# One-token attention over a long cache: each K and V load issued as two halves of its columns, one by SyncE and one by ScalarE

## The chip, the core and the metric

The kernel runs on one core of a Trainium2 chip. The core has a matrix engine (TensorE, PE in the profile), three elementwise engines (VectorE or DVE, ScalarE or ACT, GpSimd or POOL), and SyncE (SP), which here only issues DMAs. Each engine works through its own instruction queue in order; an instruction that waits on a semaphore holds everything behind it on that engine. DMA instructions stand in the same queues: SP's DMAs go to one hardware queue, ScalarE's to another, GpSimd's indirect DMAs to a third, and 16 DMA engines serve them.

The metric is the device time in microseconds (us) of one execution of the whole program. Times inside the program come from one profiled execution.

## What is computed

Two tokens (batch 2, width 512) pass a transformer block: layer norm, attention of one query position against caches of 8192 positions for 32 heads of width 128, an output projection with a residual, then a layer norm and an MLP of width 1792 with GELU, with a second residual. All is fp32. Cut to what matters:

```python
q = layernorm(x) @ wq                                # (2, 512) @ (512, 4096)
scores = einsum("bhqd,bhkd->bhqk", q, k_cache) * 128 ** -0.5
p = softmax(scores)                                  # over 8192 positions
o = einsum("bhqk,bhkd->bhqd", p, v_cache)
h = x + o.reshape(2, 4096) @ wo
out = h + mlp(layernorm(h))                          # 512 -> 1792 -> 512
```

K and V are 268 MB each; every byte is read once.

## The kernel before

**Tiles.** The work is cut into 32 steps `i` (`NI`), one for a pair of heads (`QG = 2`) and one batch entry. A step needs one K tile and one V tile, each 128 partitions by 128 positions (`NS`) by 128 floats: 64 KB of one partition, 8.39 MB in all. They come from one pool, `kv`, with three buffers (`BUFS = 3`), in the order wq, K0, V0, K1, V1, and so on. So V of step i+1 takes the buffer of K of step i and can be loaded once that K is used up; K of step i+2 takes the buffer of V of step i and can be loaded once the matmuls on that V are done. The last 'ws' tile in that pool holds the two MLP weights. All K and V loads are made by `load` (L70 to L76), called at L387, L394, L396, L409 and L411; before the change each is one DMA on SP. K of steps 30 and 31 is loaded in two parts (`parts_of`), V of step 31 in four.

**One step.** For K the tile is cut into four chunks `c` of 32 positions. VectorE multiplies a chunk in place by the query (L246). GpSimd halves part of it by an addition (L256), VectorE sums rows (L266); in the last three steps (`LAST`) ScalarE sums 38 of the 128 positions by activations with an accumulator (`by_act`, L260). When all 128 scores of each partition are there, the maximum is taken (L270), transposed on PE (L273), reduced (L277) and broadcast (L280); ScalarE makes the bias (L286) and the exponentials (L291, `exps`), and PE multiplies them with V (L314, `values`). ScalarE copies the result out (L320, `gather`).

**Around it.** Every second step, head outputs go into groups and meet rows of wo (`turn`, `turned`, L367). The groups' rows of wo are loaded by `load_wo`: five groups by a DMA on SP (L140; 1 MB, 1 MB, 1 MB, 0.5 MB and 0.25 MB), five by an indirect DMA from GpSimd (L145). The last pair's wo rows come by L412 (0.5 MB, tile 'wl' in the buffer of q). At the end: step 31 with its own order on PE (`stay_awake` L376 and `keep_warm` L515 are matmuls without use that fill gaps; `values(done, range(MOST))` L457 and the remainder of it L483), then the MLP (w1 by L468, w2 by L472).

**Order.** The framework that records the kernel decides each engine's order and adds the semaphore waits. Loads wait for the last users of their buffer. Completion of DMAs on the hardware queues is counted on eight semaphores taken in turn, so that a DMA also waits until the DMA eight before it, which has the same semaphore, has landed.

Of the kernel before, what the change touches and what calls it, by code (L numbers as in the profile page):

```python
# [41 lines left out]
def tile_decode_block(ctx: ExitStack, tc: tile.TileContext, x, k, v, wq, wo, w1, b1, w2, b2, out):  # L42
    nc = tc.nc
# [26 lines left out]
    def load(src, i, parts):  # L70
        m, b = divmod(i, B)
        t = kv.tile([P, NS, DH], F32, name="kv", tag="kv")
        rows = src[b, QG * m:QG * m + QG].rearrange("h (p j) d -> (h p) j d", j=NS)
        for s0, n in parts:
            nc.sync.dma_start(t[:, s0:s0 + n], rows[:, s0:s0 + n])
        return t  # L76

    wqt = kv.tile([P, DC, H * DH], F32, name="wqs", tag="kv")
# [16 lines left out]
    for blocks in PLAN:  # L95
        shut = blocks if isinstance(blocks, tuple) else None
        r = WR if shut else blocks
        n = (P - 4 * len(shut or ())) * r
# [286 lines left out]
    next_load = 0  # L385
    free_from = 1
    kt[0] = load(k, 0, cut(1))  # L387
    for i in range(NI):
        m, b = divmod(i, B)
        done = i - 1  # L390
        late = i == NI - 1
        if not late:
            if i < NI - 2:
                vt[i] = load(v, i, cut(1))  # L394
        else:
            vt[i] = load(v, i, [(0, 64), (64, 32), (96, 24), (120, 8)])  # L396
            b1r = rows2[:, 0].rearrange("p r q -> p (r q)")[:, :FN]
            nc.vector.memset(b1r, 0.0)
            b2s = rows2[:B, 1].rearrange("b r q -> b (r q)")
            for e in range(B):  # L400
                nc.sync.dma_start(b1r[WB * e::32], b1.rearrange("(n f) -> n f", n=NG))
            nc.sync.dma_start(b2s, b2[None, :].to_broadcast([B, D]))
# [248 lines left out]
```

## Time and profile before

| what | us |
|---|---|
| time, median of 3 runs (1307.66 to 1307.70) | 1307.67 |
| span of the profiled execution, first to last instruction | 1305.9 |
| VectorE busy | 932.7 (71%) |
| GpSimd busy | 494.2 (38%) |
| PE busy | 446.8 (34%) |
| ScalarE busy | 98.6 (8%) |
| SP's DMA queue, share of 16 DMA engines | 98.8% |
| read from memory | 562.32 MB, 431 GB/s over the span |

The profiled execution has no time of its own beside its span; the median is 1.77 us above the span. "PE so L314" is a matmul of line 314 that writes tile so; "SPq" and "ACTq" are DMA-issuing instructions of SP and ScalarE, whose lengths are those of the issue and not of the transfer. "x4" counts instructions merged in a row, and in square brackets stands how long the engine sat idle before and what ended that.

### The profile page before, as it was taken

Reading aid. Unit: us, or ns where it says so; the run is one execution under the profiler, and the core shown is the slowest. Engines: PE = TensorE matmul, PEld = TensorE weight load, DVE = VectorE, ACT = ScalarE, POOL = GpSimd, SP = SyncE. Lnnn points to the kernel's source line nnn. Section 1 sums busy time; section 2 is a strip of 40 time slices with the busy share of each in tenths; the row PEclk is TensorE's granted clock in tenths of the full one; section 3 lists DMA queues with packets and bytes.
Section 4 is the critical chain, followed back from the end, with each engine's and each line's share of the span. In section 5 each row is a group of like instructions: output and inputs, shape, how many; then the busy total and the mean of one; then the engine's idle time right before and its main releaser. Section 6 shows DMA issues by size and latency. Waiting matters only on the chain.

```text
span 1305.9 us, 7466 instructions
## 1 busy us (share of the span) xinstructions
PE 446.8 (34%) x2934; PEld 130.9 (10%) x2934; DVE 932.7 (71%) x551; ACT 98.6 (8%) x431; POOL 494.2 (38%) x151
## 2 busy tenths in 40 slices
PE   3033313333332334413342232333323334123468
PEld 0001001010010101001010010101001011000113
DVE  3666688757688666787766787666787667797891
ACT  0000000000000000000000000000000000004440
POOL 0433344532344432444332454333444433453330
PEclk9566556766566666656766566666666666566689
DMA  9999999999999999999999999999999999999998
GB/s 418 426 440 428 438 422 444 424 440 426 442 426 440 428 438 428 426 444 430 436 426 438 430 434 436 424 442 424 440 426 432 438 432 436 429 428 429 428 434 351
DMA packets 12727, 561.50 MB, mean 430 GB/s; under 512 B 1568, under 2 KB 1584, under 8 KB 2484
## 3 DMA queue, kind: packets, MB, share of 16 engines
q1 hardware_dynamic: 11968, 557.08, 98.8%
q0 software_dynamic: 720, 3.93, 0.7%
q8 instruction: 23, 0.38, 0.1%
q14 instruction: 12, 0.10, 0.0%
q10 hardware_dynamic: 4, 0.00, 0.0%
HBM read 562.32 MB, written 0.00 MB: 431 GB/s over the span
## 4 chain that ended last, share of the span: by engine, by line
DMA 43%; DVE 24%; issue 14%; PE 12%; POOL 5%; ACT 1%; SPq 0%; POOLq 0%; DVEq 0%
DMA kv<-in_A_k_cache_dram 38%; DVE kv L246 14%; PE so L314 10%; DVE s L266 9%; POOL kv L256 5%; DMA kv<-in_A_v_cache_dram 3%; DMA ws<-in_B_w_dram 1%; ACT pt L291 1%; PE rowacc L367 1%; DVE orow L350 1%; PE sm L280 1%; PE sm L273 0%; DVE gm L277 0%; DVE mx L270 0%; ACT nb L286 0%
## 5 line engine op out<-in xcount | busy, mean ns | idle before, releaser
L246 DVE TENSOR_TENSOR kv<-kv,qps 128x4096 f32<-128x4096 f32 x128 | 562.4, 4415 | 313.8 <-DMA kv<-in_A_k_cache_dram 313.6
L256 POOL TENSOR_TENSOR kv<-kv 128x2048 f32<-128x2048 f32 (+3 forms) x128 | 476.8, 3734 | 754.1 <-DVE kv L246 566.3
L266 DVE TENSOR_REDUCE s<-kv 128x32 f32<-128x2048 f32 (+5 forms) x160 | 325.3, 2066 | 10.9 <-POOL kv L256 10.6
L314 PE MATMUL so<-kv,pt 128*8 128x512 f32 x2048 | 280.8, 709 | 42.7 <-ACT pt L291 37.3
L273 PE MATMUL sm<-ident,mx 128*1 128x128 f32 x32 | 10.9, 340 | 446.0 <-DVE mx L270 446.0
L314 PEld LDWEIGHTS so<-kv,pt 128*8 128x8 f32 x2048 | 56.4, 101 | 239.5 <-issue 194.3
L367 PE MATMUL rowacc<-wog,ot 128*2 128x512 f32 x70 | 50.3, 881 | 64.8 <-DVE ot L365 33.4
L286 ACT ACTIVATE nb<-sm 128x2 f32<-128x2 f32 x32 | 5.5, 172 | 851.4 <-PE sm L280 851.4
L231 PE MATMUL qps<-q,pick 2*64 2x256 f32 x64 | 13.8, 577 | 127.6 <-DVE kv L246 127.6
L273 PEld LDWEIGHTS sm<-ident,mx 128*1 128x1 f32 x32 | 2.5, 79 | 472.5 <-issue 278.0
L358 PE MATMUL sm<-ident,orow 2*128 2x2 f32 x35 | 5.2, 244 | 130.1 <-DVE orow L350 130.1
L320 ACT ACTIVATE ss<-so 128x512 f32<-128x512 f32 x31 | 18.5, 598 | 269.6 <-PE so L314 269.6
L260 ACT ACTIVATE kv<-kv 128x128 f32<-128x128 f32 x114 | 33.5, 295 | 24.2 <-DVE kv L246 21.4
L335 PE MATMUL sm<-ss,selr 128*34 128x128 f32 x240 | 28.7, 273 | 0.0
L291 ACT ACTIVATE pt<-s,nb 64x128 f32<-64x128 f32 x64 | 25.5, 399 | 1.4
L335 PEld LDWEIGHTS sm<-ss,selr 128*34 128x34 f32 x240 | 25.1, 112 | 0.0
L260 ACT ACTIVATION_READ_ACCUMULATOR kv<-kv 128x1 f32 x114 | 21.3, 186 | 0.0
L280 PE MATMUL sm<-gm,ones 1*128 1x2 f32 x64 | 16.6, 326 | 11.9 <-DVE gm L277 11.9
L277 DVE TENSOR_REDUCE gm<-sm 1x2 f32<-1x128 f32 x32 | 8.9, 279 | 16.2 <-PE sm L273 16.2
L231 PEld LDWEIGHTS qps<-q,pick 2*64 2x64 f32 x64 | 5.5, 192 | 136.9 <-DVE kv L246 133.2
L358 PEld LDWEIGHTS sm<-ident,orow 2*128 2x128 f32 x35 | 4.4, 207 | 132.6 <-DVE orow L350 79.9
L367 PEld LDWEIGHTS rowacc<-wog,ot 128*2 128x2 f32 x70 | 6.8, 107 | 97.9 <-issue 64.1
(110 smaller groups left out, 169.2 us busy)
## 6 DMA issues: line engine op xcount, KB each, us to landing
kv<-in_A_k_cache_dram SPq DMA_DIRECT2D x4, 4096.0 KB, 32.9
ws<-in_B_w_dram SPq DMA_DIRECT2D x3, 1792.0 KB, 18.5
kv<-in_A_v_cache_dram SPq DMA_DIRECT2D x1, 4096.0 KB, 33.4
wog<-in_A_wo_dram SPq DMA_DIRECT2D x3, 1024.0 KB
kv<-in_A_v_cache_dram SPq DMA_DIRECT2D x1, 2048.0 KB, 37.9
kv<-in_A_v_cache_dram SPq DMA_DIRECT2D x1, 1536.0 KB, 41.2
ws<-in_B_w_dram SPq DMA_DIRECT2D x1, 1024.0 KB, 17.0
wog<-in_A_wo_dram SPq DMA_DIRECT2D x1, 512.0 KB
```

The costliest lines, as they stand in the source:

```text
L231: nc.tensor.matmul(t[e * HP:(e + 1) * HP, :, b], pick[32 * n:32 * n + B, b, :], rows[:, :, e], start=True, stop=True)
L246: return nc.vector.tensor_tensor(kc, kc, qb, op=ALU.mult)
L256: nc.gpsimd.tensor_tensor(t[:, :, :DH // 2], t[:, :, :DH // 2], t[:, :, DH // 2:], op=ALU.add)
L260: nc.scalar.activation(kt[i][:, j, :], kt[i][:, j, :], AF.Copy, accum_out=ST[i][:, j:j + 1])
L266: nc.vector.tensor_reduce(ST[i][:, a:e], kt[i][:, a:e, :d], axis=AX.X, op=ALU.add)
L273: nc.tensor.transpose(MT[i], mx, ident)
L280: GI[i] = nc.tensor.matmul(GM[i], ones[:1, :], gm, start=True, stop=True)
L291: nc.scalar.activation(ptz[i % 2][ps, :, 4 * e:4 * e + 4], s[ps], AF.Exp, bias=nb[ps, e:e + 1], scale=SCALE, accum_out=LT[m][ps, 32 * e + ...
L314: m = nc.tensor.matmul(so[32 * n:32 * n + 4 * QG], ptz[i % 2][:, u, :], vt[i][:, 4 * u:4 * u + 4, :], start=(u < NG), stop=(u >= NS // 4 - ...
L320: return nc.scalar.activation(SS[i], so2[i % 2], AF.Copy)
L335: nc.tensor.matmul(OP[m], sel_row[:, j, B - 1 - c:B - 1 - c + QR], SS[i - 1 + c][:, j * DH:(j + 1) * DH], start=(c == 0 and j == 0), stop= ...
L367: nc.tensor.matmul(rowacc, t[:, r, :], wo_g[g][:, r, :], start=False, stop=(g == len(groups) - 1 and r == n - 1))
```

## The change

In `load`, each part (columns s0 to s0+n of the tile) is cut in the middle. The first half is issued by SP, the second by ScalarE. The bytes, the tiles and the buffers stay the same. 64 loads in 69 DMAs become 138 DMAs, 69 in each of the two queues; one partition's piece of a whole load goes from 64 KB to 32 KB. All other DMAs stay where they were written.

```diff
         for s0, n in parts:
-            nc.sync.dma_start(t[:, s0:s0 + n], rows[:, s0:s0 + n])
+            mid = s0 + n // 2
+            nc.sync.dma_start(t[:, s0:mid], rows[:, s0:mid])
+            nc.scalar.dma_start(t[:, mid:s0 + n], rows[:, mid:s0 + n])
         return t
```

## The prediction

> **What bounds it now.** I read the page first: its DMA lines, then the windows for the rate, then the timeline around the landings of K, and last the chain and the timeline of the final 65 us.
>
> ```profile
> DMA packets 12727, 561.50 MB, mean 430 GB/s; under 512 B 1568, under 2 KB 1584, under 8 KB 2484
> q1 hardware_dynamic: 11968, 557.08, 98.8%
> q0 software_dynamic: 720, 3.93, 0.7%
> q10 hardware_dynamic: 4, 0.00, 0.0%
> ...
> 45.00:1245.00 1200.00, 388.93 (x2438) 111.43 (x2438) 887.00 (x413) 77.93 (x338) 482.06 (x138) 0.64 1.00 433
> ```
>
> SP's queue (q1) keeps the 16 DMA engines busy 98.8% of the span; from 45 to 1245 us their share is 1.00 at 433 GB/s. ScalarE's queue (q10) has carried four packets. A load of 8.39 MB so takes 19.4 us, and time is lost or won only where the DMA engines run dry or fast, and after the last bytes.
>
> ```profile
> 396.94 8.75 DVE L246 TENSOR_TENSOR kv<-kv,qps 128x4096 f32<-128x4096 f32 x2 [8.16 <-DMA kv<-in_A_k_cache_dram]
> 435.66 8.75 DVE L246 TENSOR_TENSOR kv<-kv,qps 128x4096 f32<-128x4096 f32 x2 [9.54 <-DMA kv<-in_A_k_cache_dram]
> ...
> 399.12 0.33 SPq L75 DMA_DIRECT2D kv<-in_A_k_cache_dram  x1
> 399.50 0.42 SPq L140 DMA_DIRECT2D wog<-in_A_wo_dram  x1
> 425.00 0.33 SPq L75 DMA_DIRECT2D kv<-in_A_v_cache_dram  x1
> ...
> 464.81 0.33 SPq L75 DMA_DIRECT2D kv<-in_A_v_cache_dram  x1
> ```
>
> K9 and K10 land 38.7 us apart, two loads. K9 is used up 28.1 us after landing (V10 is issued at 425.00), K10 after 29.2. When V10 is issued at 425.00, K10 has 10.7 us to run: that is the slack of the steady state.
>
> **The middle: two rings.** Both halves of a load are issued together and wait for the same things. If both rings are level, a tile lands when it did. The question is the sharing. The trace has a second ring beside SP's five times, in the indirect loads:
>
> ```profile
> DMA to landing us min/median/max: 26.0/26.2/27.6
> ...
> 234.00:258.00 24.00, 7.60 (x60) 1.62 (x52) 18.24 (x6) 0.60 (x1) 11.78 (x3) 0.71 1.01 435
> 1017.00:1041.00 24.00, 10.47 (x67) 2.24 (x67) 12.65 (x6) 1.75 (x6) 8.85 (x3) 0.67 1.03 442
> 1173.00:1197.00 24.00, 10.13 (x67) 2.38 (x67) 14.64 (x9) 7.82 (x46) 7.08 (x3) 0.71 1.00 429
> ...
> 273.00:297.00 24.00, 8.25 (x74) 3.05 (x66) 15.88 (x8) 0.60 (x1) 9.37 (x3) 0.71 1.01 437
> 1212.00:1236.00 24.00, 11.30 (x86) 3.98 (x86) 20.60 (x11) 10.10 (x64) 9.53 (x3) 0.71 1.00 427
> ```
>
> Rate: in the 24 us from each indirect load (first, best and last of five) it averages 435 GB/s, in five stretches without one (first and last shown) 434. So switching rings costs nothing to be seen. Turns: an indirect load has 720/5 = 144 packets, nine on each engine. SP's packets are 64 KB, 2.42 us at 1/16 of 433 GB/s. If the rings take turns packet by packet, nine turns cost 21.8 us, and with about 3.2 us from issue to landing that any load has (below) 25.0; measured are 26.0 to 27.6 each time, whatever SP's ring was at. So I take turns of one packet.
>
> That has a price where SP's ring carries something more. The built program puts each wo load of L140 ahead of K's first half on SP, while ScalarE's ring goes on. Let z be the landing of V9, both rings level. SP holds 1 MB of wo (eight packets of 8 KB on each engine) and then K10's first half; ScalarE holds K10's second half (eight of 32 KB). Packet by packet both are through at z + 2.4 + 9.7 = z + 12.1. V10 was issued at z - 19.4 + 28.1 and flows 3.2 later, z + 11.9; its second half now takes every other turn, and K10's first half lands at z + 12.1 + 19.4 = z + 31.5, 9.7 late. K10 is used up 29.2 later, and V11 flows at z + 31.5 + 29.2 + 3.2 = z + 63.9. All that was issued ahead of it (wo, K10, V10, K11) is through at z + 2.4 + 58.1 = z + 60.5. The engines stand idle 3.4 us; then the rings are level again. The 1 MB loads ahead of K10 and K16 give 3.4 each. Smaller ones are through before V's half flows, and SP catches up alone: 0.5 MB ahead of K24 gives 1.2 (1.0 us alone, and L412's load, which the build moves there, fills 1.2), 0.25 MB ahead of K28 1.8 (1.6 alone). The first wo load falls into the start, where K2 is issued near 94 and SP is alone for 2.7 us; 0.5 by the same reckoning. **Sum 10.3 us**, bounds 0 and 5 x 3.4 = 17.
>
> **The start.**
>
> ```profile
> 0.74 0.40 SPq L79 DMA_DIRECT2D wqs<-in_A_wq_dram  x1
> 23.34 9.51 PE L216 MATMUL so<-wqs,yT 128*2 128x512 f32 x64 [15.16 <-DMA wqs<-in_A_wq_dram]
> 42.64 8.75 DVE L246 TENSOR_TENSOR kv<-kv,qps 128x4096 f32<-128x4096 f32 x2 [28.54 <-DMA kv<-in_A_k_cache_dram]
> 70.65 0.33 SPq L75 DMA_DIRECT2D kv<-in_A_v_cache_dram  x1
> 82.12 8.75 DVE L246 TENSOR_TENSOR kv<-kv,qps 128x4096 f32<-128x4096 f32 x2 [10.44 <-DMA kv<-in_A_k_cache_dram]
> ```
>
> wq, 8.39 MB, lands 22.6 us after issue: 3.2 beyond its 19.4. ScalarE's K0 and V0 halves now flow beside wq and K0's first half, so K0 lands 9.7 late, at 52.3, and wq at 33; the query needs 11 more and is in time. K0 is used up at 80.3, V1 flows at 83.5. K1 (82.1, the same bytes as before) and the wo load behind it last until 84.5. Price 0; with that cover gone it would be the 1.4 us from 82.1.
>
> **ScalarE's queue.** A DMA costs it 0.4 us of issue, beside waits that are there anyway: V's half stands just ahead of the bias L286, which needs the same maximum; K's half ahead of `gather`, which needs the same matmuls. Price 0 for 29 steps. In the last three the eight semaphores bite. The exponentials of step 28 come behind the first `by_act` of step 29, 12 us late, and those of step 29 wait for K30's first quarter, some 4 us; K30 is then issued near 1200 and V30 near 1226, with V29 in flight until 1204 and K31 until 1244: hidden. What is not hidden: ScalarE's fourth V31 half must wait until V30's first half has **landed**, and behind it in ScalarE's queue stand the exponentials of step 30 and all 38 sums of step 31.
>
> ```profile
> 1243.20 0.17 ACT L286 ACTIVATE nb<-sm 128x2 f32<-128x2 f32 x1 [3.68 <-PE sm L280]
> 1247.14 0.31 ACT L260 ACTIVATE kv<-kv 128x128 f32<-128x128 f32 x1 [2.74 <-issue]
> 1249.78 0.29 ACT L260 ACTIVATE kv<-kv 128x128 f32<-128x128 f32 x1
> 1265.27 0.29 ACT L260 ACTIVATE kv<-kv 128x128 f32<-128x128 f32 x1
> ...
> 1244.45 0.38 PE L298 MATMUL sm<-ls,ones 128*128 128x2 f32 x2 [1.29 <-ACT pt L291]
> 1253.04 9.07 PE L376 MATMUL spare<-ones,s 128*22 128x512 f32 x16 [8.20 <-DVE s L266]
> 1264.06 4.48 PE L314 MATMUL so<-kv,pt 128*8 128x512 f32 x40 [1.96 <-DMA kv<-in_A_v_cache_dram]
> 1268.47 0.27 PE L273 MATMUL sm<-ident,mx 128*1 128x128 f32 x1
> ...
> 1269.42:1285.95 16.53, 15.74 (x124) 4.88 (x124) 4.10 (x10) 3.23 (x8) 0.00 (x0) 1.00 0.98 412
> 1285.95:1302.90 16.95, 14.26 (x229) 8.02 (x229) 3.58 (x10) 3.10 (x5) 0.00 (x0) 1.00 0.89 372
> ...
> 1293.75 1.71 PE L590 MATMUL so<-ws,ones 128*32 128x448 f32 x16 [0.48 <-DMA ws<-in_B_w_dram]
> 1298.14 1.74 PE L620 MATMUL po<-ws,pt 128*32 128x128 f32 x56 [1.26 <-DMA ws<-in_B_w_dram]
> 1300.55 1.08 PE L620 MATMUL po<-ws,pt 128*32 128x128 f32 x32 [0.68 <-DMA ws<-in_B_w_dram]
> 1301.79 1.07 PE L620 MATMUL po<-ws,pt 128*32 128x128 f32 x24 [0.16 <-DMA ws<-in_B_w_dram]
> ...
> 1242.83 42.02 DMA kv<-in_A_v_cache_dram
> 1284.87 16.88 DMA ws<-in_B_w_dram
> ```
>
> In the chain of waits the end is bytes: V31 until 1284.87, the MLP weights until 1301.75. V30 lands at T = 1264.06. Before, ScalarE did its step-31 sums from 1247.14 to 1265.6; now it starts at T. Issue 0.4, bias 0.2, one sum 0.3, exponentials 1.1: T + 2.0. The 37 other sums at (1249.78 - 1247.14)/9 = 0.29 each: T + 12.9. PE is later still: the total L298 (T + 2.4) now stands after one of the eight idle matmuls of L376, so seven eighths of 9.07 follow (T + 10.3), then the 4.48 of step 30's V (T + 14.8), and only then the transposed maximum L273. PE's work of the window 1269.42 to 1285.95 starts 0.95 later, T + 15.8, and its 15.74 us are now without a wait for V31: end T + 31.5 = 1295.6, **9.6 late**. The stretch to 1302.90 no longer waits for weights, which are there before: 0.48 at L590, and L620 takes its 3.89 of busy time in place of 1298.14 to 1302.86: 0.8. **Price 9.6 - 1.3 = 8.3 us.** L412's 0.5 MB, now ahead of V30, put T another **1.2 us** back.
>
> **Sum.** 10.3 + 8.3 + 1.2 = 19.8 on the span of 1305.9: 1325.7. The median of the runs is 1.77 above that span: **1327.5 us**. A difference under 0.2% (2.6 us) is about what cannot be told from none. Own range of this case: gaps 5 to 17, the tail 2 either way as PE or ScalarE ends last: 1320 to 1336.
>
> **Rivals.** *Turns of a whole half load.* If a ring keeps its turn for all its nine packets of a load, wo and K10's second half delay nothing for K10's first, no gaps open, and the time is 1327.5 - 10.3 = 1317.2; with the indirect windows' 435 for 434 GB/s some 3 less. Against it: an indirect load would then land at once after the load in progress, at varying times and not 26.0 to 27.6 always. The Trainium skill, page "DMA: Bandwidth & Descriptors", section "Queues, rings and completion order", has each engine drain a whole packet of 9 to 17 descriptors before it switches rings, which is this rival if a descriptor is one of the profile's packets. Chance 0.20.
>
> *Two rings run faster.* The one window at 442 GB/s had two rings. At that rate the 1200 us at 433 shrink by 24.4, and 1327.5 becomes 1303; it decides from 440 GB/s, where 19.8 are regained. Against it: the five such windows average 435. The Trainium skill, same page, section "Issuing engines are not separate DMA queues", says that DMAs from several engines interleave on the same 16 and only issue time is saved; by it this gain is none, and the sum stays. Chance 0.06, faster.
>
> *Switching costs.* 26.0 less 25.0 over 18 switches bounds it at 0.06 us on each 1.21 us packet; a fifth of it, 0.011, is 0.9% or 12 us: 1339. The windows speak against it. Chance 0.08.
>
> *The wait is not in the way.* If ScalarE passes its fourth half early and the rings stay level, nothing is left but 1.2 us: 1309. Chance 0.04, no difference.
>
> **Numbers.** Forecast 1327.5, chance 0.62. The range 1313 to 1337 takes in it and the whole-load turns (0.82). Faster 0.06, same 0.04, slower 0.90.
>
> **What would show it.** K10 (and K16, K24, K28, each behind a wo load) landing some 10 us late in the timeline, and V11 issued with an idle DMA stretch of 1 to 3 us behind it; K0's multiply near 52; ScalarE idle until V30 lands, its step-31 sums all after that, L273 some 15 us after V30; the weights' landing no longer in the chain. Wrong: level landings of K10, a steady rate off 433 by over 1%, or step-31 sums before V30's landing.

## Result: 22 us slower, and the profile after

| | before | after |
|---|---|---|
| time, median (us) | 1307.67 (1307.66 to 1307.73) | 1329.66 (1327.64 to 1330.91) |
| ratio, 95% interval | | 1.0165 (1.0155 to 1.0176) |
| span of the profiled execution (us) | 1305.9 | 1328.2 |

The changed kernel is 22.0 us, or 1.65%, slower. Its lines in the profile stand two higher from the change on: the multiplication is L248, SP's half L76, ScalarE's half L77, the wo load L142, the bias L288.

First the DMA lines of the page and the window from 45 to 1245 us (PE, PEld, DVE, ACT and POOL busy, PE's granted clock, DMA share, GB/s):

```profile
DMA packets 22663, 561.50 MB, mean 423 GB/s; under 512 B 2672, under 2 KB 2688, under 8 KB 3972
q1 hardware_dynamic: 11968, 288.65, 50.9%
q10 hardware_dynamic: 9940, 268.44, 47.0%
...
45.00:1245.00 1200.00, 375.51 (x2413) 108.51 (x2413) 874.27 (x400) 72.05 (x305) 480.19 (x137) 0.64 1.00 429
```

The two queues now share the bytes almost evenly. The same bytes come in nearly twice as many packets, and the long window has fallen from 433 to 429 GB/s: 4/433 of 1200 us is 11 us. The other half of the loss must lie at the end.

The timeline of the changed kernel around two wo loads (K9, K10 and the issue of V11; K15, K16 and the issue of V17):

```profile
397.21 0.33 SPq L142 DMA_DIRECT2D wog<-in_A_wo_dram  x1
400.82 8.75 DVE L248 TENSOR_TENSOR kv<-kv,qps 128x4096 f32<-128x4096 f32 x2 [8.76 <-DMA kv<-in_A_k_cache_dram]
447.02 8.75 DVE L248 TENSOR_TENSOR kv<-kv,qps 128x4096 f32<-128x4096 f32 x2 [17.01 <-DMA kv<-in_A_k_cache_dram]
475.23 0.33 SPq L76 DMA_DIRECT2D kv<-in_A_v_cache_dram  x1
...
636.43 8.75 DVE L248 TENSOR_TENSOR kv<-kv,qps 128x4096 f32<-128x4096 f32 x2 [8.56 <-DMA kv<-in_A_k_cache_dram]
687.49 8.75 DVE L248 TENSOR_TENSOR kv<-kv,qps 128x4096 f32<-128x4096 f32 x2 [21.92 <-DMA kv<-in_A_k_cache_dram]
715.70 0.33 SPq L76 DMA_DIRECT2D kv<-in_A_v_cache_dram  x1
```

K9 and K10 were 38.7 us apart before; they are 46.2 apart now, and K15 and K16 51.1. The windows of 12 us behind the issues of V11, V17, V25 and V29 show what the lateness costs:

```profile
470.00:482.00 12.00, 6.05 (x35) 2.57 (x39) 9.18 (x7) 1.15 (x5) 1.25 (x1) 0.55 0.98 407
710.00:722.00 12.00, 5.58 (x27) 2.43 (x31) 11.47 (x10) 1.15 (x5) 2.44 (x2) 0.50 0.85 344
1030.00:1042.00 12.00, 7.73 (x41) 1.89 (x45) 9.96 (x9) 1.15 (x5) 4.42 (x3) 0.70 0.98 393
1190.00:1202.00 12.00, 3.80 (x14) 1.00 (x18) 11.36 (x11) 2.33 (x13) 4.95 (x3) 0.50 0.86 350
```

Against 430 GB/s the four windows lack 12 x (1 - 407/430) = 0.6, 2.4, 1.0 and 2.2 us of transfer, 6.3 in all.

The end, from the timeline, with the last rows of the chain of waits behind it:

```profile
1253.92 25.54 ACTq L77 DMA_DIRECT2D kv<-in_A_v_cache_dram  x4
1279.51 0.17 ACT L288 ACTIVATE nb<-sm 128x2 f32<-128x2 f32 x1 [27.07 <-DMA kv<-in_A_v_cache_dram]
1294.27 0.27 PE L275 MATMUL sm<-ident,mx 128*1 128x128 f32 x1
1321.75 3.26 PE L622 MATMUL po<-ws,pt 128*32 128x128 f32 x112 [1.07 <-DVE pt L619]
...
1239.88 39.22 DMA kv<-in_A_v_cache_dram
1281.49 8.13 PE spare L378 x13
```

ScalarE's four V31 halves take 25.54 us to issue, until 1279.46: the last waits until V30's first half has landed, at 1279.10 (the chain's 1239.88 + 39.22). The bias that ScalarE gave at 1243.20 before comes at 1279.51. From there on the chain has no DMA: the MLP weights, which ended the kernel before, are there long before they are needed (L622 waits for VectorE).

### The profile page after: what moved, and what is told of

It reads as the page before. It is cut to its first block, busy times and chain, and to the rows that moved or that the text cites. A ratio compares the mean times of both kernels' runs of the same rounds, so it can differ in the third digit from the quotient of the medians.

```text
span 1328.2 us, 7584 instructions
## 1 busy us (share of the span) xinstructions
PE 442.0 (33%) x2934; PEld 131.6 (10%) x2934; DVE 930.6 (70%) x551; ACT 98.0 (7%) x431; POOL 495.4 (37%) x151
## 4 chain that ended last, share of the span: by engine, by line
DMA 48%; DVE 28%; PE 17%; POOL 4%; issue 2%; ACT 1%; ACTq 0%; POOLq 0%; DVEq 0%
DMA kv<-in_A_k_cache_dram 42%; DVE kv L248 15%; DVE s L268 12%; PE so L316 11%; POOL kv L258 4%; DMA kv<-in_A_v_cache_dram 3%; DMA wqs<-in_A_wq_dram 2%; PE rowacc L369 2%; ACT pt L293 1%; PE spare L378 1%; PE so L218 1%; PE sm L282 1%; PE sm L275 0%; DVE orow L352 0%; PE sm L337 0%
## 5 line engine op out<-in xcount | busy, mean ns | idle before, releaser
L248 DVE TENSOR_TENSOR kv<-kv,qps 128x4096 f32<-128x4096 f32 x128 | 562.6, 4414 | 330.2 <-DMA kv<-in_A_k_cache_dram 330.1
L316 PE MATMUL so<-kv,pt 128*8 128x512 f32 x2048 | 270.4, 684 | 43.2 <-ACT pt L293 40.6
L275 PE MATMUL sm<-ident,mx 128*1 128x128 f32 x32 | 11.8, 368 | 407.1 <-DVE mx L272 407.1
L288 ACT ACTIVATE nb<-sm 128x2 f32<-128x2 f32 x32 | 5.5, 172 | 884.5 <-PE sm L282 857.4
L233 PE MATMUL qps<-q,pick 2*64 2x256 f32 x64 | 13.8, 577 | 109.6 <-DVE kv L248 109.6
L275 PEld LDWEIGHTS sm<-ident,mx 128*1 128x1 f32 x32 | 2.5, 79 | 422.8 <-issue 222.5
L337 PE MATMUL sm<-ss,selr 128*34 128x128 f32 x240 | 36.7, 303 | 11.4 <-ACT ss L322 10.7
L337 PEld LDWEIGHTS sm<-ss,selr 128*34 128x34 f32 x240 | 26.8, 124 | 15.4 <-ACT ss L322 14.1
L146 POOL MEMSET wog<- 128x2048 f32 x5 | 9.0, 1805 | 51.0 <-PE rowacc L369 51.0
L279 DVE TENSOR_REDUCE gm<-sm 1x2 f32<-1x128 f32 x32 | 8.9, 278 | 14.6 <-PE sm L275 13.5
```

Source lines behind the costliest of these rows:

```text
L233: nc.tensor.matmul(t[e * HP:(e + 1) * HP, :, b], pick[32 * n:32 * n + B, b, :], rows[:, :, e], start=True, stop=True)
L248: return nc.vector.tensor_tensor(kc, kc, qb, op=ALU.mult)
L275: nc.tensor.transpose(MT[i], mx, ident)
L316: m = nc.tensor.matmul(so[32 * n:32 * n + 4 * QG], ptz[i % 2][:, u, :], vt[i][:, 4 * u:4 * u + 4, :], start=(u < NG), stop=(u >= NS // 4 - ...
L337: nc.tensor.matmul(OP[m], sel_row[:, j, B - 1 - c:B - 1 - c + QR], SS[i - 1 + c][:, j * DH:(j + 1) * DH], start=(c == 0 and j == 0), stop= ...
```

## Experiments

The theory after the result: 4 to 5 us of smaller packets or of two rings, 6 to 8 of gaps behind the wo loads, about 8.7 of ScalarE's blocked queue at the end, 1.2 of L412's load. The main rival: one loss of rate everywhere, of which the late tiles and the late end are only the image. Every ratio below is against the kernel before.

**One ring, two halves.** ScalarE's half is issued by SP.

```diff
-            nc.scalar.dma_start(t[:, mid:s0 + n], rows[:, mid:s0 + n])
+            nc.sync.dma_start(t[:, mid:s0 + n], rows[:, mid:s0 + n])
```

> Every load of K and V is still two halves of the columns, but SP issues both, so one ring carries everything again and ScalarE issues none of them. Theory (the loss is two rings out of step, about 8 us of gaps, 4.5 us of slower transfer and 8.7 us of a blocked ScalarE queue at the end): all of it goes away but what the smaller packets cost by themselves; span 1306 to 1309, time 1308 to 1311. K's landings 38.7 us apart. Rival A (halving the packets costs the rate, whatever the ring): K's landings stay 38.85 us apart and the time is about 1312 to 1313. Rival B (SP's issuing is a limit): more instructions on SP delay the loads, time above 1315, SP's waits before the loads of K and V no longer the longest.

Measured: 1313.08 us (1312.96 to 1313.15), ratio 1.0041 (1.0027 to 1.0055). The gaps and the late end are gone, but 5.4 us stay: rival A. So the loss of rate does not need a second ring.

**Four quarters, one ring.** This doubles the suspect.

```diff
-            mid = s0 + n // 2
-            nc.sync.dma_start(t[:, s0:mid], rows[:, s0:mid])
-            nc.scalar.dma_start(t[:, mid:s0 + n], rows[:, mid:s0 + n])
+            for j in range(4):
+                at, w = s0 + j * n // 4, n // 4
+                nc.sync.dma_start(t[:, at:at + w], rows[:, at:at + w])
```

> Every load of K and V in four quarters of the columns, all issued by SP: one ring, pieces of 16 KB. Theory (each piece of a partition has a fixed cost on its DMA engine: 32 KB pieces made K's landings 38.85 us apart instead of 38.71, sixteen more pieces on an engine for two loads, 9 ns each): 48 more than before, landings 39.1 us apart, time 1307.6 + 3 x 5.4 = 1322 to 1326. Rival A (the 5.4 of the halves came of something that happens once per DMA or of the smaller last parts, not of the pieces): 1313 to 1317. Rival B (the eight semaphores, now two tiles' worth, hold back SP): above 1328, with idle DMA engines in the windows.

Measured: 1326.11 us (1325.71 to 1326.48), ratio 1.0139 (1.0122 to 1.0156), 18.3 us over the 1307.77 of the kernel before in the same runs. The multiplication's first waits for K2 and K27 in the kernel before, with halves and with quarters on SP:

```profile
120.69 8.75 DVE L246 TENSOR_TENSOR kv<-kv,qps 128x4096 f32<-128x4096 f32 x2 [9.38 <-DMA kv<-in_A_k_cache_dram]
1106.38 4.42 DVE L246 TENSOR_TENSOR kv<-kv,qps 128x4096 f32<-128x4096 f32 x1 [8.29 <-DMA kv<-in_A_k_cache_dram]
```

```profile
111.34 8.76 DVE L248 TENSOR_TENSOR kv<-kv,qps 128x4096 f32<-128x4096 f32 x2 [9.62 <-DMA kv<-in_A_k_cache_dram]
1100.73 4.42 DVE L248 TENSOR_TENSOR kv<-kv,qps 128x4096 f32<-128x4096 f32 x1 [8.06 <-DMA kv<-in_A_k_cache_dram]
```

```profile
107.19 4.42 DVE L248 TENSOR_TENSOR kv<-kv,qps 128x4096 f32<-128x4096 f32 x1 [10.02 <-DMA kv<-in_A_k_cache_dram]
1104.31 4.42 DVE L248 TENSOR_TENSOR kv<-kv,qps 128x4096 f32<-128x4096 f32 x1 [8.71 <-DMA kv<-in_A_k_cache_dram]
```

25 steps take 985.69, 989.39 and 997.12 us. A step has 256 pieces of 64 KB, 16 on each of the 16 DMA engines. Halves add 16 to each, quarters 48: 3.70/(25 x 16) is 9.3 ns a piece, 11.43/(25 x 48) is 9.5. Three times the added pieces, three times the cost: about 9.4 ns for each. The DMAs multiply as the pieces do, so these times alone can't tell a cost of the piece from one of the DMA. The records of single packets in the traces can. From 100 to 1100 us of these three runs a packet of 64 KB takes 2.420 us in the median, one of 32 KB 1.215 and one of 16 KB 0.613: two halves take 10 ns more than the whole, four quarters 32. What a DMA has of its own on each engine, a packet of 4 bytes, takes 9 ns, so the two DMAs that halves add to a step are at most 18 ns of the 148 (3.70 us in 25 steps) by which it is longer. Of the 18.3 us some 14.6 are these pieces over all 32 steps (11.43 x 32/25). Most of the rest is a gap near the end, where two windows of 6 us, from 1294 to 1306, have 347 and 315 GB/s: SP issues V31's quarters until 1296.4, and the MLP weights only behind them. (The first half lands some 9 us before a whole tile would, which is why the rows begin earlier; it gains nothing, since bytes are the bound.)

**One transfer of 138.** Only the last part of V31 (8 of its columns of 128 floats) is issued whole, by SP.

```diff
+            if n == 8:
+                nc.sync.dma_start(t[:, s0:s0 + n], rows[:, s0:s0 + n])
+                continue
```

> As the changed kernel, except that one transfer of all, the last 0.5 MB part of the last V, is issued whole by SP instead of in halves. Theory (ScalarE's last half is held till the second part of V30 has landed, with 38 reductions of step 31 and the exps of step 30 behind it): the end comes 7 to 9 us earlier, time 1320 to 1323, ScalarE's last load is issued some 15 us earlier than 1279 and the first row sum no longer waits for it. The landings of K up to step 30 stay as in the changed kernel. Rival A (the tail is late only since everything ahead of it landed late; the queue costs nothing): no change, 1328 to 1331. Rival B (the smaller packets and two rings at the end are what costs): no change either, since only one transfer differs.

Measured: 1321.0 us (1319.92 to 1322.61), ratio 1.0106 (1.0089 to 1.0123): 8.7 us less than the changed kernel, for a quarter of a MB moved to the other queue. Of the 10.1 us between the two profiled spans (1328.2 and 1318.1), 7.8 lie behind the landing of V30 (1279.10 and 1276.75). The other 2.3 were there before: K28 lands 2.5 us earlier (1162.53 and 1165.01), in a stretch that the edit does not touch, and that is scatter between executions. In the timeline ScalarE's last V31 halves are now issued by 1259.5 and not 1279.5, and the bias waits for PE:

```profile
1250.98 8.49 ACTq L80 DMA_DIRECT2D kv<-in_A_v_cache_dram  x3
1259.92 0.17 ACT L291 ACTIVATE nb<-sm 128x2 f32<-128x2 f32 x1 [10.44 <-PE sm L285]
```

Both rivals expected no change. A load that waits in a computing engine's queue holds up the arithmetic behind it: shown.

**The last three steps on SP.**

```diff
+            if i >= NI - LAST:
+                nc.sync.dma_start(t[:, s0:s0 + n], rows[:, s0:s0 + n])
+                continue
```

> As the changed kernel, except that K and V of the last three steps are issued whole by SP, so ScalarE has no load among the exps and sums of the end. Theory (blocked ScalarE queue at the end is about 8.7 us): 1319 to 1322; the first row sum comes with the exps, as in the kernel before; K's landings up to step 28 as in the changed kernel. Rival A (the tail is late only since everything ahead of it is): 1327 to 1331. Against the run with one transfer changed: the same within 2 us if the one blocked transfer is all; earlier by more if ScalarE's other late loads of the end cost too.

Measured: 1320.18 us (1319.62 to 1320.95), ratio 1.0096 (1.0079 to 1.0112). Ten more transfers whole on SP change another 0.8 us: the one blocked transfer is nearly all of it.

**Wo loads on both rings.** Each wo load is cut in halves, one on each queue.

```diff
-            nc.sync.dma_start(t[:, :r], wo[r0:r0 + n, :].rearrange("(p r) n -> p r n", r=r))
+            rows = wo[r0:r0 + n, :].rearrange("(p r) n -> p r n", r=r)
+            h, w = (r // 2, D) if r > 1 else (r, D // 2)
+            nc.sync.dma_start(t[:, :h, :w], rows[:, :h, :w])
+            nc.scalar.dma_start(t[:, r - h:r, D - w:], rows[:, r - h:, D - w:])
```

> As the changed kernel, except that the five weight loads that SP alone issued between the loads of K and V are also cut in halves over both rings, so that neither ring gets ahead of the other. Theory (SP's ring falls behind by the time of these loads, and the tile that is then late holds up the next load of V): K10, K16, K24 and K28 land about 10 us earlier than in the changed kernel, and the gaps of some 8 us go; time 1320 to 1323, the tail's 8.7 us stays. Rival A (the gaps come of the rings' drifting by themselves, whatever the weights): K's late landings remain somewhere else, time 1327 to 1331. Rival B (whole-ring loss of rate): landings still 38.85 us apart in undisturbed stretches with both theories, but with B alone nothing is gained.

Measured: 1326.86 us (1326.63 to 1327.48), ratio 1.0148 (1.0131 to 1.0165): only 2.8 us less than the changed kernel, where 7 to 9 were expected. K10, K16, K24 and K28 are in time, but K2 and K25 land 10 us late. The program's order tells why: ScalarE's half of the first wo load was placed ahead of V0, SP's behind K1, and L412's load still stands on SP alone, ahead of K25. The rings were not level. This run gives a test of the turns that had not been planned. Timeline of its start, with wq's landing and K0's:

```profile
4.59 0.33 ACTq L145 DMA_DIRECT2D wog<-in_A_wo_dram  x1
4.96 0.46 ACTq L77 DMA_DIRECT2D kv<-in_A_v_cache_dram  x1
31.84 9.60 PE L221 MATMUL so<-wqs,yT 128*2 128x512 f32 x64 [17.54 <-DMA wqs<-in_A_wq_dram]
43.86 8.75 DVE L251 TENSOR_TENSOR kv<-kv,qps 128x4096 f32<-128x4096 f32 x2 [29.36 <-DMA kv<-in_A_k_cache_dram]
```

In the changed kernel these were:

```profile
31.91 9.60 PE L218 MATMUL so<-wqs,yT 128*2 128x512 f32 x64 [17.62 <-DMA wqs<-in_A_wq_dram]
51.30 8.75 DVE L248 TENSOR_TENSOR kv<-kv,qps 128x4096 f32<-128x4096 f32 x2 [36.80 <-DMA kv<-in_A_k_cache_dram]
```

Half a MB more on the other ring makes K0 come 7.4 us **earlier**. With turns of one piece that is what must happen: on each DMA engine the eight pieces of K0's first half now take turns with eight of wo's of 4 KB and not with eight of V0's of 32 KB. 4.19 + 0.52 MB at 433 GB/s are 10.9 us from wq's landing, 42.7 (measured 43.86); 4.19 + 4.19 MB are 19.4, 51.3 (measured 51.30). Turns of a whole load, beginning with wq, would land wq at 22.6 and K0 at 42.0 in both. If ScalarE's K0 half had gone ahead of wq, whole turns would give much the same as single pieces (32.3, then 43.2 and 51.7), so these rows alone don't settle it. The halves' own times do more. The page's list of DMA issues for this run, with the median from issue to landing last:

```profile
kv<-in_A_v_cache_dram SPq DMA_DIRECT2D x31, 4096.0 KB, 31.5
kv<-in_A_v_cache_dram ACTq DMA_DIRECT2D x31, 4096.0 KB, 30.3
kv<-in_A_k_cache_dram SPq DMA_DIRECT2D x30, 4096.0 KB, 37.5
kv<-in_A_k_cache_dram ACTq DMA_DIRECT2D x30, 4096.0 KB, 36.2
```

The two halves are issued together and land 1.2 and 1.3 us apart in the median, about one piece of 32 KB (1.21 us). With whole turns one half would land 9.7 ahead of the other. The packet records of the changed kernel show the turns themselves. From the first to the last of the 128 packets of 8 KB of the wo load ahead of K16 (652.85 to 666.04), SP's queue sent 133 packets and ScalarE's 138 of 32 KB: one each in turn, whatever their size.

**Level rings.** Now the wo halves are placed behind the same step's K half on both queues, L412's load behind V30, and the last three steps are on SP. `sp[0]` and `act[0]` are the last load of K or V on each queue.

```diff
+            with tc.issue_after(sp[0].ins):
+                nc.sync.dma_start(t[:, :h, :w], rows[:, :h, :w])
+            with tc.issue_after(act[0].ins):
+                nc.scalar.dma_start(t[:, r - h:r, D - w:], rows[:, r - h:, D - w:])
...
+            with tc.issue_after(sp[0].ins):
+                nc.sync.dma_start(wl, wo[HL * DH:, :].rearrange("(h p) n -> p h n", p=P))
```

> K and V of the last three steps whole on SP, the five wo loads cut in halves over both rings, each half behind the same step's K half, and L412's load behind V30 again as before. So both rings carry the same bytes in the same order up to step 28 and ScalarE has no load at the end; two rings and 32 KB packets stay. Theory (tail 8.7, gaps about 6, L412's load 1.2, and smaller packets 5.4, the last being what the run with both halves on SP cost): only the packets are left, 1312 to 1314, no K lands 9 us late behind a wo load. Rival A (two rings have a price of their own, or ScalarE's waits in the steady state delay something): above 1315. Rival B (the late K tiles have nothing to do with wo): K10, K16, K24 or K28 still land late, about 1318.

Measured: 1313.47 us (1313.34 to 1314.23), ratio 1.0044 (1.0028 to 1.0061). Only the pieces are left, and two rings cost nothing besides: K2 to K27 take 989.64 us here and 989.39 with one ring.

```profile
122.38 8.75 DVE L258 TENSOR_TENSOR kv<-kv,qps 128x4096 f32<-128x4096 f32 x2 [11.00 <-DMA kv<-in_A_k_cache_dram]
1112.02 4.42 DVE L258 TENSOR_TENSOR kv<-kv,qps 128x4096 f32<-128x4096 f32 x1 [8.20 <-DMA kv<-in_A_k_cache_dram]
...
1249.15 42.00 DMA kv<-in_A_v_cache_dram
1291.16 16.78 DMA ws<-in_B_w_dram
```

The last two rows are from the chain: V31 and the MLP weights set the end again.

**The mirror image.** The wo loads and L412's load are issued by ScalarE, all else as in the changed kernel.

```diff
-            nc.sync.dma_start(t[:, :r], wo[r0:r0 + n, :].rearrange("(p r) n -> p r n", r=r))
+            nc.scalar.dma_start(t[:, :r], wo[r0:r0 + n, :].rearrange("(p r) n -> p r n", r=r))
...
-            nc.sync.dma_start(wl, wo[HL * DH:, :].rearrange("(h p) n -> p h n", p=P))
+            nc.scalar.dma_start(wl, wo[HL * DH:, :].rearrange("(h p) n -> p h n", p=P))
```

> As the changed kernel, but the five wo loads and L412's load are issued by ScalarE instead of SP, all else the same: the mirror image. Now the other ring lags, so K's second half is late and its first in time. Theory (a gap comes only when VectorE has to wait; it reaches the second half some 13 us after the first, more than the lag of 9.7): no gaps behind K10, K16, K24 and K28, the first halves of K land in time; the tail's 8.7 and the packets' 5.4 stay: 1322 to 1325. At the start K0 lands near 45 instead of 51, since the eight small packets of wo take turns with K0's first half. Rival (unequal rings cost the same whichever lags): 1328 to 1331.

Measured: 1323.04 us (1318.81 to 1323.53), ratio 1.0109 (1.0091 to 1.0127): 6.6 us less. The timeline shows K10's two halves, and the windows no gap where V11 and V17 left one:

```profile
429.56 8.75 DVE L248 TENSOR_TENSOR kv<-kv,qps 128x4096 f32<-128x4096 f32 x2 [3.34 <-DMA kv<-in_A_k_cache_dram]
450.51 4.42 DVE L248 TENSOR_TENSOR kv<-kv,qps 128x4096 f32<-128x4096 f32 x1 [9.42 <-DMA kv<-in_A_k_cache_dram]
...
470.00:482.00 12.00, 8.89 (x68) 1.99 (x66) 10.75 (x5) 0.82 (x3) 7.92 (x2) 0.88 1.00 431
710.00:722.00 12.00, 9.78 (x63) 3.31 (x67) 11.47 (x8) 1.15 (x5) 4.57 (x1) 0.64 1.00 426
```

K10's first half lands at 429.56 (447.02 in the changed kernel), the second 20.95 later, a lag that is larger than the 13 us I had counted on as cover. VectorE does wait, yet it has begun so much earlier that V11 is issued at 467.32 and not at 475.23, and finds the DMA engines busy. In these runs unequal rings cost only where the half that VectorE needs first is the late one.

**Wo behind K.** SP's wo load stands behind K's half in SP's queue, L412's load behind V30.

```diff
+            with tc.issue_after(sp[0].ins):
+                nc.sync.dma_start(t[:, :r], wo[r0:r0 + n, :].rearrange("(p r) n -> p r n", r=r))
...
+            with tc.issue_after(sp[0].ins):
+                nc.sync.dma_start(wl, wo[HL * DH:, :].rearrange("(h p) n -> p h n", p=P))
```

> As the changed kernel, but SP's wo loads are placed behind the same step's K half in SP's queue instead of ahead of it, and L412's load behind V30 as before: the bytes, rings and packets are those of the changed kernel. Theory (the harm is that K's first half is the late one; a V that lands 9.7 us late is needed only when its exponentials are there, some 10 us after): the gaps of about 6 and the 1.2 of L412's load go, tail and packets stay: 1321 to 1324, K10, K16, K24 and K28 land no later than their neighbours. Rival (any lag of one ring costs, since the late V holds its buffer and the next K): 1326 to 1330.

Measured: 1335.44 us (1334.43 to 1336.66), ratio 1.0214 (1.0196 to 1.0231): 5.8 us more than the changed kernel. My theory for this run fell. K10 is in time, but the lag is not worked off while both rings have work: it passes from V10 to K11, which now is the late tile, and V12, issued 28.5 us after it, leaves the gap. (By the packet records SP's half of V10 ends 18.2 us behind ScalarE's, those of K11 and V11 16.8, that of K12 9.7 and that of V12 no more, once ScalarE's ring has run dry.) Timeline and window:

```profile
491.96 4.42 DVE L251 TENSOR_TENSOR kv<-kv,qps 128x4096 f32<-128x4096 f32 x1 [21.86 <-DMA kv<-in_A_k_cache_dram]
520.45 0.33 SPq L78 DMA_DIRECT2D kv<-in_A_v_cache_dram  x1
...
510.00:522.00 12.00, 2.71 (x11) 1.20 (x11) 11.41 (x8) 0.00 (x0) 4.53 (x2) 0.50 0.84 339
```

K9 to K10 is 38.9 us there, K10 to K11 51.1. K29, late by the wo load that stands behind K28, lands 48.0 us after K28, at 1207.66, and leaves another gap, of 5 us, in the window from 1218 to 1224 (71 GB/s): ScalarE's first sum of step 29, at 1212.11, stands ahead of the exponentials of step 28, and K30, which needs the buffer of V28, is issued at 1221.99.

**Two small edits together.** The one transfer and the mirror image (both diffs above).

> The changed kernel with the two small edits together: the last 0.5 MB of V31 whole on SP, and the wo loads and L412's load issued by ScalarE. Theory (the tail and the gaps add up): 1329.7 - 8.7 - 6.6 = 1314.4, so 1312.5 to 1316, what the smaller packets leave. Rival (what is won in one place is lost to the other, both being waits for the same bytes): 1317 to 1323.

Measured: 1315.86 us (1314.81 to 1318.31), ratio 1.0066 (1.005 to 1.0083). The two gains add up to 13.8 of the expected 15.3 us. They are two losses, not one seen twice.

**64 KB pieces on two rings.** This was meant to tell pieces from rings: as the level rings, but each half is 64 partitions with whole rows.

```diff
-            sp[0] = nc.sync.dma_start(t[:, s0:mid], rows[:, s0:mid])
-            act[0] = nc.scalar.dma_start(t[:, mid:s0 + n], rows[:, mid:s0 + n])
+            h = P // 2
+            sp[0] = nc.sync.dma_start(t[:h, s0:s0 + n], rows[:h, s0:s0 + n])
+            act[0] = nc.scalar.dma_start(t[h:, s0:s0 + n], rows[h:, s0:s0 + n])
```

> As the run with level rings, but each half is 64 of the 128 partitions instead of half of the columns, so that one partition's piece is 64 KB again on both rings. Theory (the slower rate comes of the smaller packets and not of two rings): K's landings 38.7 us apart instead of 38.85, 1307.5 to 1310. Rival (switching between rings costs): still 38.85 us apart and 1312 to 1314. Second rival (a DMA of 64 partitions does not reach all 16 engines evenly): clearly above 1314.

Measured: 2447.61 us (2430.06 to 2471.85), ratio 1.8651 (1.8573 to 1.8729). It tells nothing of its question, so it was followed by one that does tell why: the kernel before, with partition halves, both on SP.

```diff
-            nc.sync.dma_start(t[:, s0:s0 + n], rows[:, s0:s0 + n])
+            for p0 in (0, P // 2):
+                nc.sync.dma_start(t[p0:p0 + P // 2, s0:s0 + n], rows[p0:p0 + P // 2, s0:s0 + n])
```

> The kernel before, with each load of K and V as two halves of the partitions, 64 each, both issued by SP: one ring, pieces of 64 KB. It tells why the level rings with halves of the partitions took 2448 us. Theory (a transfer to 64 partitions alone runs at half the rate, whatever the ring): about twice the time, 2300 to 2500, at 210 to 230 GB/s with the DMA engines busy all the time. Rival (two rings that write to different partitions get in each other's way): 1308 to 1315.

Measured: 2679.31 us (2677.97 to 2680.64), ratio 2.0488 (2.0447 to 2.0529). Windows of both, two rings first:

```profile
100.00:1100.00 1000.00, 164.28 (x1039) 49.27 (x1039) 370.81 (x168) 23.39 (x78) 204.74 (x56) 0.57 1.00 213
```

```profile
100.00:1100.00 1000.00, 170.05 (x1016) 49.84 (x1020) 345.53 (x157) 21.00 (x72) 190.12 (x53) 0.57 1.00 207
```

The DMA engines are busy all the time at half the rate, with one ring as with two. The Trainium skill, page "SBUF — State Buffer", section "Can I just issue two DMAs to hit both halves?", says that a transfer reaches all the ports of the memory only if it spans all 128 partitions, and that two transfers to the two halves serialize. The trace agrees: 207 GB/s for 433 on one ring, and 213 with the halves on two.

## Why the prediction was right: by its own steps

The forecast was 1327.5 and 1329.66 was measured. The sign and the two mechanisms were right. Two terms were mis-sized, the gaps by some 4 us too much and the pieces by 5.4 too little, and it is luck that these errors nearly cancel.

| term (us) | predicted | shown by the runs |
|---|---|---|
| gaps behind the wo loads | 10.3 | 6.6 (mirror image); 6.3 in the windows |
| ScalarE's blocked queue at the end | 8.3 | 8.7 (one transfer); 7.3 behind V30's landing in the traces |
| smaller pieces | 0 | 5.4 (both halves on SP) |
| L412's load moved | 1.2 | not separated (the mirror image moves it too) |
| sum | 19.8 | 20.7 of 22.0; 1.3 left, about L412's 1.2 |

**Turns of one piece: borne out.** K16 was computed to land 31.5 us after V15; with V15 counted 19.4 behind K15, at 655.8, K16 comes 31.7 later, at 687.49. K0 was computed for 52.3 (measured 51.30) and wq for 33 (31.91). The rival of whole-load turns expected no late K and no gaps, and gaps of 6.3 us are there; the halves of a load land 1.2 us apart and not 9.7, and 133 packets of one queue went beside 138 of the other. The Trainium skill's rule that stood beside that rival (page "DMA: Bandwidth & Descriptors", section "Queues, rings and completion order": a packet of 9 to 17 descriptors is drained before the ring changes) does not fit that 1.2, if a descriptor is one of the profile's packets.

**The gaps: mechanism right, size too large.** Computed were 3.4, 3.4, 1.2, 1.8 and 0.5; the windows lack 0.6, 2.4, 1.0, 2.2 and nothing at the start. V17 was issued 28.2 us after K16's landing, where I took the 29.2 of K10 before: that is the 1.0 missing there. At K10 a step of the sum failed. K10 lands 26.8 after V9, counted as above for 420.2: 4.7 earlier than computed. In the sum V10's half takes over on ScalarE's ring where K10's ends (z + 11.9 against z + 12.1). By the packet records K10's half ends there at 429.07, and V10, issued at 428.89, begins at 432.30: for 3.2 us SP's ring had the engines to itself. At K16 the break is 0.4 us, and K16 came as computed. The break comes of "both rings level", which left out that the 16 engines are not level among themselves: the last packet of K9's first half ended at 400.34 on the slowest engine and by 396.71 on 14 of the 16, so that z, counted from K9's landing, was too late for most of them. The other 1.5 of the 4.7 stays open.

**Switching costs nothing: right for rings, and yet the term was wrong.** I asked only what a second ring costs, and it costs nothing (989.64 against 989.39). The step that failed is that a load cut in two was given the cost of its bytes alone. Pieces of 32 KB for 64 KB cost 9.4 ns each, 5.4 us over the whole kernel. The rival "switching costs" had a price of that sign but the wrong cause: it asked for it in the windows with two rings, and the indirect loads' windows, at 435 against 434 GB/s, rightly showed none.

**The tail: right in its mechanism, 1 us too large.** T, the landing of V30, is 1279.10, and L275, computed for T + 14.8, comes at 1294.27, T + 15.2. Behind T 49.1 us follow, and 41.8 before the change: 7.3 where 8.3 was computed. The predicted order, eight semaphores, then a blocked issue, then 38 sums behind it, is what the rows show, and one transfer undoes it. T itself is 15.0 later than before, where the sum had 11.5; the gaps (6.3), the pieces (some 4.7) and L412's load (1.2) explain 12.2 of it. The packet records show most of the rest. When V30's last packet ends (1263.3 before, 1278.0 after, 14.7 later), 545.52 MB have been moved before the change and 546.96 after it, and 1.4 MB are 3.3 us at 433 GB/s, in place of the 1.2 for L412's load: on the two rings parts of V31 flow while the last pieces of V30 are still on their way. That explains 14.3 of the 14.7.

**ScalarE's waits in the first 29 steps cost nothing: right.** With level rings ScalarE still issues its halves there, and the time is that of one ring.

## What to carry to other kernels

Where one queue already kept the DMA engines at 100%, a second had nothing to win: cutting each load added 9.4 ns a piece, made the order of landing depend on what else stands in each ring, and put waits into the queue of an engine that computes. If two rings are to be used, give both the same pieces in the same order, and if that cannot be, let the ring with the extra load be the one whose half is needed last. Look at the last steps first: a load that waits there for a semaphore holds the arithmetic behind it, and whether one transfer of 0.5 MB was cut was worth 7 to 9 us.

## What the runs showed of the hardware

Cutting pieces of 64 KB into 32 or 16 KB costs some 9.4 ns for each added piece, in proportion over 16 and 48 of them, and the packets' own times show it (10 and 32 ns more for the same 64 KB). Two rings share by pieces and not by bytes: 133 packets, nearly all of 8 KB, went on one while 138 of 32 KB went on the other, and 0.5 MB more in 4 KB pieces on the other ring made K0 land 7.4 us earlier. A ring's lag is not worked off while both rings have work; it passes to the next tile. Transfers to 64 partitions ran at 207 to 213 GB/s with the DMA engines busy all the time. And the time varied more in most runs whose rings are not level: by 3.3 us in the changed kernel, 4.7 in the mirror image and 2.2 with wo behind K, against 0.9 with level rings and 0.1 to 0.6 us for the kernel before. The run with the wo loads on both rings, not level either, varied by 0.9 only, so with four or five executions each this is a hint and no more.
